# Attention plus two expert layers on one core: queries and keys loaded with doubled rows and split in place, instead of split once and moved by DMA

## The chip, the core and the metric

The kernel runs on one core of one Trainium2 chip. The metric is device time in microseconds (us) of one execution, start to end; lower is better. The engines are named as in the profile: PE (TensorE, matmuls), DVE (VectorE), ACT (ScalarE), POOL (GpSimd) and SP (SyncE, which here issues nearly all DMAs, in order).

## What is computed

The reference, cut to what matters:

```python
# q, k, v: (4, 8, 576, 64): batch, heads, sequence, head size
scores = np.matmul(q, k.transpose(0, 1, 3, 2)) / np.sqrt(64)
thresh = np.max(scores, axis=-1, keepdims=True) - tau
scores = np.where(scores >= thresh, scores, -1000000000.0)
attn = np.exp(scores - np.max(scores, axis=-1, keepdims=True))
attn = attn / (np.sum(attn, axis=-1, keepdims=True) + 1e-09)
x = np.matmul(attn, v)                         # then to (2304, 512)
g = x @ w_gate                                 # 512 -> 1536
x = (g / (1 + np.exp(-g)) * (x @ w_val)) @ w_out
h = np.maximum(x @ w_in, 0.0)                  # 512 -> 2048
x = (h * h) @ w_out2
```

Everything is float32. A matmul in full float32 is replaced by passes over parts: a number is split into a high part, rounded to the format fp32r that PE reads, and a low part, the rest, and the products high x high, high x low and low x high are summed.

## The kernel before

**Stages.** Attention over 4 batches of 8 heads comes first. The heads are taken in 16 pairs, and a pair has nine tiles of 128 queries (ORDER, L642): four of head a, one that holds the last 64 queries of both heads (T), four of head b. That makes 144 tiles. The first layer's gate and value matmuls of finished batches run between the tiles as fill (`work`, L872: every tile adds 2600 columns to a credit that fill may use up; what is left runs on PE alone behind the last tile). Behind that comes the rest of the two layers, which is not touched by the change.

**One tile.** `QK` (L652) multiplies queries with keys into PSUM. A query tile has 128 rows of contraction: 64 rows of high parts of the scaled queries and 64 rows of low parts (`qs`); the keys stand as `kh` (high parts twice) and `kl` (low parts twice), so two matmuls for each half of the 576 keys give all the products. `RED` (DVE) takes the row maximum, `CUT` and `EXP` (ACT) threshold and exponentiate with a row sum, `RCP` (DVE, L696) inverts it, `NORM` (POOL, L700) scales. In batches 1 to 3 NORM writes a 16-bit high part, `LO` (DVE, L751) the low part beside it, `XT` (L759) is a transposing DMA issued on SP, and `AV` (L763) multiplies with the values, fourteen matmuls for each of four parts of a pair. In batch 0 the tiles are transposed on PE and copied by DVE and ACT instead. In batches 1 to 3, `rs`, the reciprocal times a constant, is made by a one-column instruction on POOL right before NORM.

**Buffers.** EXP's results (`es`, L445) turn over three buffers in batch 0 and two in batches 1 to 3, where the third is one of NORM's three 16-bit buffers (`both`, L447).

**A pair's preparation** (`pair_steps`, L586) is a generator that is advanced one step per tile while the pair before is worked on. One load of 896 KB brings q, k and v of both heads into `raw` (one buffer), with 64 rows per head. ACT scales the queries into the high part and copies the keys into theirs (`land`); DVE takes the low queries, POOL the low keys in two halves, in place. Then `move`, once for each head, issues six DMAs on SP that put high and low rows where `qs`, `kh` and `kl` want them, each 64 rows to 64 rows, 144 KB. For head a it also moves the low keys of both heads into one joint tile `kd` and the high queries of the T tile into `qd`, a block diagonal, so that the T tile needs three matmuls a half and not four (L655 to L661). `tail` (L482) copies the T tile's 64 queries from `qs` into `qt` on POOL. `values` (L510) splits the values in batches 1 to 3: POOL copy, POOL subtraction, POOL copy, POOL subtraction for each head.

The first pair (`first_pair`, L524) loads each head's rows twice from a second input and splits in place.

**What sets the order.** The code is emitted tile by tile in the loop at the end; the offsets in the table `early` (L1693) put a step ahead of or behind others. Each engine and SP then work in their fixed order, an instruction waiting for its inputs holding all behind it.

Of the kernel before, what the change touches and what calls it, by code (L numbers as in the profile page):

```python
# [22 lines left out]
P = 128  # L23
# [15 lines left out]
RAWW = 2 * S + 2 * VW  # L39
# [45 lines left out]
def attention_moe(tc, qkv, qk0, tau, w1, w2, out, cfg):  # L85
# [361 lines left out]
    both = [es[-1].bitcast(F16)[:, : 2 * S], *(ptp.tile([P, 2 * S], F16, name=f"both{j}", tag=f"both{j}") for j in range(2))]  # L447
# [17 lines left out]
    qds = [ptp.tile([P, P], F32R, name=f"qd{i}", tag=f"qd{i}") for i in range(1)]  # L465
# [35 lines left out]
    def whole_values(h):  # L501
        hd = heads[h]
        if any(whole(h // 2, i) for i, x in PARTS.items() if x[2] == hd["odd"]):
            c0 = 5 * 640 + h % 4 * (VW + D)
            hd["vf"] = flat[:, c0 : c0 + VW + D]
            c0 += hd["odd"] * D
            a = 2 * S + hd["odd"] * VW
            nc.sync.dma_start(flat[:, c0 : c0 + VW], qkv[h // 2, :, a : a + VW])

    def values(hd, h, raw):  # L510
# [4 lines left out]
        v = raw[:, 2 * S + odd * VW : 2 * S + (odd + 1) * VW].rearrange("p (c d) -> p c d", d=D)  # L515
# [8 lines left out]
    def first_pair():  # L524

        raw = load_pair(0)
        for h in range(2):
            r = raw if h == 0 else rawp.tile([P, 2 * S], F32, name="raw01", tag="land")
            if h:
                for c in (0, S):  # L530
                    nc.sync.dma_start(r[:, c : c + S], qk0[h, :, c : c + S])
            else:

                for c in (slice(0, P), slice(S, 2 * S), slice(P, S)):
                    nc.sync.dma_start(r[:, c], qk0[h, :, c])
# [42 lines left out]
            def s2():  # L578
                tail(hd)
                values(hd, h, raw)  # L580
# [5 lines left out]
    def pair_steps(p):  # L586

        raw = load_pair(p)
        land = rawp.tile([P, 2, S], F32R, name=f"land{p}", tag="land")
        q, k = raw[:, 0:S], raw[:, S : 2 * S]  # L590
        qh, kh = land[:, 0], land[:, 1]

        def move(h):
            hd = head(h)
            rows = slice(hd["odd"] * D, (hd["odd"] + 1) * D)
            for dst, parts_ in (
                (hd["qs"], (qh, q.bitcast(F32R))),
                (hd["kh"], (kh, kh)),
                (hd["kl"], (k.bitcast(F32R), k.bitcast(F32R))),
            ):  # L600
                for j, src in enumerate(parts_):
                    nc.sync.dma_start(dst[j * D : (j + 1) * D, :].bitcast(F32), src[rows, :].bitcast(F32))
            tail(hd)
            if not hd["odd"]:
                hd["qd"], hd["kd"] = qds[0], qp.tile([P, S], F32R, name=f"kd{p}", tag="kd", bufs=1)
                nc.sync.dma_start(hd["kd"].bitcast(F32), k)
                for c in (slice(0, D), slice(D, P)):
                    nc.sync.dma_start(hd["qd"][c, c].bitcast(F32), qh[c, 4 * P : S].bitcast(F32))
# [12 lines left out]
        yield None
        ops.sub(cfg["kl"], k[:, :HS].bitcast(F32R), k[:, :HS], kh[:, :HS].bitcast(F32))
# [29 lines left out]
    def QK(t):  # L652
# [36 lines left out]
    def EXP(t):  # L689
        e = es[t % (len(es) if t < 9 * NPAIR else len(es) - 1)]  # L690
# [221 lines left out]
    for i in range(NTILE + late):  # L912
# [39 lines left out]
        if i == 4:  # L952
            with tc.issue_after(st[2]["norm"]):
                for x_ in qds:
                    nc.gpsimd.memset(x_.bitcast(F32), 0.0)
# [671 lines left out]
def pack(inputs):  # L1627
# [96 lines left out]
```

## Time and profile before

| | |
|---|---|
| median of 3 runs | 1229.49 us (1227.45 to 1229.86) |
| the profiled execution | 1229.54 us; its span from first to last instruction 1227.8 us |
| mean granted PE clock | 0.968 of full |
| busy, share of the span | PE 91%, DVE 72%, ACT 50%, POOL 25% |
| DMA | 179.90 MB, 147 GB/s |

The profile is of one execution. A busy time is that of an engine's instructions without waits; PE's is overstated where matmuls overlap. A wait is charged to what ended it. The granted clock is the share of full speed that PE was given: 1.00 is 2.4 GHz, 0.5 is 1.2 GHz. POOL has no work behind the attention, so its 25% of the span falls into the first 541 us.

### The profile page before, as it was taken

How to read it: one execution, taken by the hardware profiler on the slowest of the kernel's cores; microseconds unless marked ns; L12 is line 12 of the kernel's file. 1: busy time of each engine (PE TensorE's matmuls, PEld its weight loads, DVE VectorE, ACT ScalarE, POOL GpSimd, SP SyncE). 2: the span in 40 equal slices, each digit the busy share in tenths (PEclk: the TensorE clock that was granted, in tenths of full speed). 3: DMA queues.
4: the chain of work that ended last, by engine and by line, in shares of the span. 5: the costliest groups of instructions: out<-in, count | busy, mean ns of one | idle time of the engine just before them, and what ended most of it. 6: DMA issues, size and time to landing. Idle time of an engine off the chain costs nothing.

```text
span 1227.8 us, 18958 instructions
## 1 busy us (share of the span) xinstructions
PE 1113.4 (91%) x6194; PEld 965.7 (79%) x6194; DVE 887.3 (72%) x2088; ACT 615.1 (50%) x1377; POOL 307.8 (25%) x524
## 2 busy tenths in 40 slices
PE   7998877667878877899999999999999999999998
PEld 6776766456667765799888888889889899889997
DVE  7888865765676757659998687878765858867554
ACT  7886644455554545535543343434555545554232
POOL 5577755654555646310000000000000000000000
PEclk9999988789989899999999999999999999999999
DMA  7768867777897787613222013436435444544452
GB/s 209 217 180 201 192 137 157 142 162 160 166 174 169 154 164 159 127 36 99 89 80 85 17 44 120 146 118 223 184 147 185 166 155 158 183 155 151 177 182 92
DMA packets 188258, 179.90 MB, mean 147 GB/s; under 512 B 138112, under 2 KB 139392, under 8 KB 188160
## 3 DMA queue, kind: packets, MB, share of 16 engines
q1 hardware_dynamic: 188016, 178.70, 54.4%
q8 instruction: 49, 0.80, 0.3%
q14 instruction: 49, 0.40, 0.1%
q10 hardware_dynamic: 144, 0.00, 0.0%
HBM read 93.06 MB, written 22.28 MB: 94 GB/s over the span
## 4 chain that ended last, share of the span: by engine, by line
PE 55%; POOL 14%; issue 9%; DMA 8%; DVE 8%; SPq 3%; ACT 3%; POOLq 0%; DVEq 0%; ACTq 0%
PE mm L258 16%; PE mm L1532 15%; PE mm L1479 11%; PE mm L300 7%; DMA raw<-in_qkv_dram 3%; POOL both L707 3%; POOL raw L78 3%; PE bank L258 2%; DMA qs<-raw 2%; POOL e L707 2%; DMA wr<-in_w_dram 2%; PE bank L780 1%; POOL vs L74 1%; POOL rs L706 1%; DVE st__114 L677 1%
## 5 line engine op out<-in xcount | busy, mean ns | idle before, releaser
L677 DVE TENSOR_SCALAR_CACHE_REDUCE st__114<-s,tau_c 128x576 bf16<-128x576 f32 x144 | 116.7, 811 | 36.8 <-PE s L667 25.9
L685 ACT ACTIVATE z<-s,thr 128x576 f32<-128x576 f32 x144 | 106.3, 738 | 48.9 <-DVE st__114 L677 40.6
L693 ACT ACTIVATE e<-z 128x577 f32<-128x577 f32 x144 | 98.5, 684 | 60.0 <-DVE r L698 38.8
L258 PE MATMUL mm<-xs,wa 128*128 128x512 f32 (+2 forms) x672 | 125.7, 347 | 0.5 <-ACT x L70 0.5
L258 PEld LDWEIGHTS mm<-xs,wa 128*128 128x128 f32 x672 | 109.4, 188 | 15.7 <-ACT x L70 0.7
L258 PE MATMUL bank<-xs_m,wa 128*128 128x288 f32 x576 | 100.2, 316 | 19.4 <-DVE xs_m L78 11.6
L780 PE MATMUL bank<-pt,vs 128*128 128x256 f16 (+1 forms) x432 | 76.5, 321 | 40.7 <-DMA pt<-both 21.2
L755 DVE SCALAR_TENSOR_TENSOR both<-e,rs,both 128x512 f16<-128x512 f32 (+1 forms) x144 | 85.6, 635 | 37.5 <-POOL both L707 37.2
L667 PE MATMUL s<-kh,qs 128*128 128x288 f32 x256 | 88.0, 361 | 24.9 <-ACT z L685 14.3
L258 PEld LDWEIGHTS bank<-xs_m,wa 128*128 128x128 f32 x576 | 86.2, 200 | 25.7 <-DVE xs_m L78 13.9
L780 PEld LDWEIGHTS <-vs 128*128 128x128 bf16 x432 | 41.2, 107 | 61.9 <-issue 28.4
L667 PEld LDWEIGHTS s<-kh,qs 128*128 128x128 f32 x256 | 50.5, 200 | 41.4 <-ACT z L685 26.0
L667 PE MATMUL s<-kl,qs 128*128 128x288 f32 x256 | 74.6, 312 | 3.7 <-DMA kl<-raw 3.7
L258 PE MATMUL mm<-xs,wb 128*128 128x512 f32 (+1 forms) x360 | 74.9, 368 | 0.0
L1549 DVE TENSOR_TENSOR xF<-xF,mm 128x512 f32<-128x512 f32 x54 | 36.9, 684 | 51.0 <-PE mm L1532 50.9
L258 PEld LDWEIGHTS mm<-xs,wb 128*128 128x128 f32 x360 | 62.8, 188 | 11.3
L755 DVE SCALAR_TENSOR_TENSOR e<-e,rs,e 128x512 f16<-128x512 f32 x72 | 47.2, 696 | 29.9 <-POOL e L707 29.8
L1532 PE MATMUL mm<-wb,wx 128*128 128x512 f32 x270 | 67.2, 389 | 0.0
L70 ACT ACTIVATE wb<-wf 128x256 fp32r<-128x256 f32 x82 | 34.0, 414 | 65.5 <-DVE wf L1134 38.4
L1479 PE MATMUL mm<-right,wb 128*128 128x384 f32 x348 | 65.3, 335 | 0.8 <-DVE right L78 0.8
L1131 ACT ACTIVATE wf<-wr 128x256 f32<-128x256 f32 x64 | 27.6, 433 | 69.6 <-DMA wr<-in_w_dram 49.3
L1479 PEld LDWEIGHTS mm<-right,wb 128*128 128x128 f32 x348 | 60.8, 188 | 1.5 <-DVE right L78 1.0
(163 smaller groups left out, 2645.7 us busy)
## 6 DMA issues: line engine op xcount, KB each, us to landing
wr<-in_w_dram SPq DMA_DIRECT2D x106, 256.0 KB, 3.0
raw<-in_qkv_dram SPq DMA_DIRECT2D x15, 896.0 KB, 5.9
kh<-land SPq DMA_DIRECT2D x60, 144.0 KB, 2.7
kl<-raw SPq DMA_DIRECT2D x60, 144.0 KB, 2.9
xF<-in_w_dram SPq DMA_DIRECT2D x30, 256.0 KB, 3.2
right<-kept1T SPq DMA_DIRECT2D x8, 768.0 KB, 5.5
right<-kept0T SPq DMA_DIRECT2D x7, 768.0 KB, 5.4
right<-kept SPq DMA_DIRECT2D x6, 768.0 KB, 4.3
```

The lines of the kernel that those rows point to most:

```text
L258: mm(pt[:, :n], w[:, a, col + c * P : col + (c + 1) * P], xs[:, b, c, :], start=(i == 0), stop=(i == len(TERMS) - 1),)
L300: mm(pt[:, :n], ws[k][:, a, 2 * DM + m * P : 2 * DM + (m + 1) * P], us[k][:, b, :], start=(k == 0 and i == 0), stop=(k == ahead and i == 2),)
L667: mm(sp[:, cols], l, r[:, cols], start=(n_ == 0), stop=(n_ == len(pairs) - 1),)
L677: red = nc.vector.tensor_scalar(st_, st[t]["s"][:, :S], scalar1=tau_c, scalar2=None, op0=ALU.subtract, op1=ALU.max, accum_out=th)
L685: nc.scalar.activation(z[:, :S], st[t]["s"][:, :S], AF.Prelu, bias=st[t]["thr"], scale=-1.0, alpha=1 / SLOPE)
L693: ex = nc.scalar.activation(e, st[t]["z"], AF.Exp, scale=-SLOPE, accum_out=sum_)
L707: norm = nc.gpsimd.tensor_scalar(a[:, :S], e, scalar1=rs, scalar2=1.0, op0=ALU.mult, op1=ALU.mult)
L755: nc.vector.scalar_tensor_tensor(a[:, to : to + c.stop - c.start], e[:, c], r, a[:, c], op0=ALU.mult, op1=ALU.subtract)
L780: mm(o[:, :n], v, pt[:, k if k < 9 else k - 9, lo : lo + n], start=(k == 0), stop=(k == 13))
L1479: mm(bank[:, :BK], w[:, a, c * P : (c + 1) * P], t[:, b, c, :], start=(n == 0 and x in ("11", "12", "S1")), stop=(n == 5), skip_group_chec ...
L1532: mm(pt, u[:, b, s * P : (s + 1) * P], w[a], start=(half == 0 and j == 0 and i == 0), stop=(half == 1 and j == 1 and i == 2),)
L1549: nc.vector.tensor_tensor(acc[:, j, :], acc[:, j, :], pt, op=ALU.add)
```

## The change

The host lays out q and k for each head with its 64 rows twice (128 rows of 1152 floats), and v in an input of its own. Each head is loaded by itself, 576 KB, into a buffer of its own, and v of a pair, 320 KB, in batches 1 to 3. The high queries are made on all 128 rows by POOL in batch 0 and by ACT behind it; DVE turns the second 64 rows into low parts; ACT copies the high keys, POOL subtracts the low keys in two halves, for each head and on 128 rows. No DMA moves anything inside the chip; `kd`, `qd` and `land` go, and the T tile has four matmuls a half. EXP has three buffers throughout and NORM three of its own. `rs` is made on DVE behind the reciprocal. The two value copies of a head go from POOL to ACT.

The diff, cut to its core:

```diff
-    both = [es[-1].bitcast(F16)[:, : 2 * S], *(ptp.tile([P, 2 * S], F16, name=f"both{j}", tag=f"both{j}") for j in range(2))]
+    both = [ptp.tile([P, 2 * S], F16, name=f"both{j}", tag=f"both{j}") for j in range(3)]
...
-    def load_pair(p):
-        raw = rawp.tile([P, RAWW], F32, name=f"raw{p}", tag="raw")
-        if p:
-            nc.sync.dma_start(raw, qkv[p])
-        return raw
+    def raw_head(h):
+        return rawp.tile([P, 2 * S], F32, name=f"raw{h}", tag=f"raw{h % 2}")
...
     def pair_steps(p):
...
-        yield None
-        if cfg["qs"] == "A":
-            nc.scalar.activation(qh, q, AF.Copy, scale=qscale)
...
-        ops.sub(cfg["kl"], k[:, HS:].bitcast(F32R), k[:, HS:], kh[:, HS:].bitcast(F32))
-        move(2 * p)
...
+        raws = [raw_head(2 * p + j) for j in range(2)]
+        rawv = None
+
+        def query(j):
+            hd, q = head(2 * p + j), raws[j][:, :S]
+            if p < NPAIR:
+                nc.gpsimd.tensor_scalar(hd["qs"], q, scalar1=qscale, scalar2=1.0, op0=ALU.mult, op1=ALU.mult)
+            else:
+                nc.scalar.activation(hd["qs"], q, AF.Copy, scale=qscale)
+
+        def key(j):
+            hd, q = heads[2 * p + j], raws[j][:, :S]
+            ops.copy(cfg["kh"], hd["kh"], raws[j][:, S:])
+            low = hd["qs"][D:, :]
+            nc.vector.scalar_tensor_tensor(
+                low, q[D:, :], qscale[D:, :], low.bitcast(F32), op0=ALU.mult, op1=ALU.subtract
+            )
+
+        def key_low(j, c):
+            hd = heads[2 * p + j]
+            ops.sub(cfg["kl"], hd["kl"][:, c], raws[j][:, S:][:, c], hd["kh"][:, c].bitcast(F32))
+
+        halves_ = (slice(0, HS), slice(HS, S))
+        nc.sync.dma_start(raws[0], qk[2 * p])
+        yield None
+        nc.sync.dma_start(raws[1], qk[2 * p + 1])
+        if not all(whole(p, i) for i in PARTS):
+            rawv = rawp.tile([P, 2 * VW], F32, name=f"rawv{p}", tag="rawv")
+            nc.sync.dma_start(rawv, values_[p])
+        yield None
+        query(0)
+        yield None
+        key(0)
+        yield None
+        key_low(0, halves_[0])
+        yield None
+        key_low(0, halves_[1])
+        tail(heads[2 * p])
+        yield None
+        values(heads[2 * p], 2 * p, rawv)
+        query(1)
+        yield "next"
+        key(1)
+        key_low(1, halves_[0])
+        yield None
+        key_low(1, halves_[1])
+        tail(heads[2 * p + 1])
+        values(heads[2 * p + 1], 2 * p + 1, rawv)
+        yield None
...
-            pairs = [(hd["qt"][:], hd[x_]) for hd in (ha, hb) for x_ in ("kh", "kl") if x_ == "kh" or "kd" not in ha]
-            if "kd" in ha:
-                pairs.append((ha["qd"], ha["kd"]))
+            pairs = [(hd["qt"][:], hd[x_]) for hd in (ha, hb) for x_ in ("kh", "kl")]
...
-        e = es[t % (len(es) if t < 9 * NPAIR else len(es) - 1)]
+        e = es[t % len(es)]
...
     def RCP(t):
         r = st[t]["r"] = sm.tile([P, 1], F32, name=f"r{t}", tag="r")
         nc.vector.reciprocal(r, st[t]["sum"])
+        if way(t) == "VV":
+            rs = st[t]["rs"] = sm.tile([P, 1], F32, name=f"rs{t}", tag="rs")
+            nc.vector.tensor_scalar(rs, r, scalar1=UNIT, scalar2=None, op0=ALU.mult)
...
-            rs = st[t]["rs"] = sm.tile([P, 1], F32, name=f"rs{t}", tag="rs")
-            nc.gpsimd.tensor_scalar(rs, r, scalar1=UNIT, scalar2=1.0, op0=ALU.mult, op1=ALU.mult)
+            rs = st[t]["rs"]
...
-    "vh": "P",
+    "vh": "A",
```

## Rows read from the trace of the kernel before

**Rows 1.** Windows: length, busy us of PE, weight loads, DVE, ACT, POOL; clock, DMA.
```profile
496.40:514.60 18.20, 15.62 (x107) 13.27 (x108) 14.26 (x39) 12.48 (x27) 9.04 (x19) 1.00 0.67 122
0.00:95.00 95.00, 82.34 (x480) 70.17 (x481) 77.65 (x210) 80.26 (x184) 59.41 (x102) 1.00 0.72 204
95.00:521.00 426.00, 330.33 (x2078) 272.56 (x2077) 295.91 (x699) 223.68 (x498) 243.21 (x415) 0.91 0.79 161
521.00:541.00 20.00, 19.58 (x148) 19.32 (x146) 7.21 (x16) 5.99 (x16) 5.19 (x8) 1.00 0.01 2
541.00:1227.80 686.80, 681.14 (x3492) 603.69 (x3492) 506.50 (x1164) 305.21 (x680) 0.00 (x0) 1.00 0.39 134
```
**Rows 2.** PE in order of time: start, length, line, count.
```profile
364.82 1.77 PE L300 MATMUL bank<-m_u,wa 128*128 128x288 f32 x12
```

**Rows 3.** POOL in order of time: NORM of tiles 36, 135 and 143.
```profile
95.64 0.79 POOL L707 TENSOR_SCALAR both<-e,rs 128x576 f16<-128x576 f32 x1
...
496.40 0.75 POOL L707 TENSOR_SCALAR both<-e,rs 128x576 f16<-128x576 f32 x1
...
514.58 0.75 POOL L707 TENSOR_SCALAR e<-e,rs 128x576 f16<-128x576 f32 x1
```

**Rows 4.** POOL in order of time at the end of a pair.
```profile
377.73 0.74 POOL L707 TENSOR_SCALAR e<-e,rs 128x576 f16<-128x576 f32 x1
...
389.14 0.24 POOL L74 TENSOR_SCALAR qt<-qs 128x64 fp32r<-128x64 f32 x1 [6.37 <-DMA qs<-raw]
...
390.81 0.75 POOL L707 TENSOR_SCALAR both<-e,rs 128x576 f16<-128x576 f32 x1
```

**Rows 5.** SP's queue in order of time, the same stretch.
```profile
381.56 1.24 SPq L602 DMA_DIRECT2D kl<-raw  x2
...
386.50 0.59 SPq L602 DMA_DIRECT2D qs<-raw  x1
```

**Rows 6.** Waits, 95 to 521 us: who for whom, total us, times, longest.
```profile
POOL rs L706 <- DVE r L698: 78.7, 72, 2.6
...
POOL qt L74 <- DMA qs<-raw: 50.0, 8, 9.1
```

**Rows 7.** ACT by line and shape, 95 to 521 us: busy us, mean ns, idle before.
```profile
L70 ACT ACTIVATE xs_m<-xF 128x288 fp32r<-128x288 f32 x21 | 8.6, 431 | 3.8 <-PE bank L258 3.8
L612 ACT ACTIVATE land<-raw,qscale 128x576 fp32r<-128x576 f32 x11 | 8.5, 773 | 7.7 <-DMA raw<-in_qkv_dram 7.0 <-issue 0.6
...
L70 ACT ACTIVATE land<-raw 128x576 fp32r<-128x576 f32 x11 | 7.4, 669 | 0.0
```

**Rows 8.** DVE and POOL by line and shape, the same columns.
```profile
L618 DVE SCALAR_TENSOR_TENSOR raw<-raw,qscale,land 128x576 fp32r<-128x576 f32 x11 | 10.8, 980 | 4.1 <-ACT land L612 4.1
...
L547 DVE SCALAR_TENSOR_TENSOR qs<-raw,qscale,qs 64x576 fp32r<-64x576 f32 x1 | 0.8, 818 | 0.0
...
L536 DVE TENSOR_SCALAR qscale<-tau_t 128x1 f32<-128x1 f32 x1 | 0.2, 153 | 1.7 <-DMA tau_t<-in_tau_dram 1.7
...
L706 POOL TENSOR_SCALAR rs<-r 128x1 f32<-128x1 f32 x108 | 23.1, 213 | 82.1 <-DVE r L698 78.7 <-ACT e L693 1.9 <-ACT z L685 1.1
...
L78 POOL TENSOR_TENSOR raw<-raw,land 128x288 fp32r<-128x288 f32 x22 | 22.0, 1018 | 0.0
...
L561 POOL TENSOR_SCALAR qs<-raw,qscale 128x576 fp32r<-128x576 f32 x1 | 0.7, 746 | 3.1 <-DMA raw<-in_qk_dram 3.1
```

**Rows 9.** DVE's LO in the last pair; LO and POOL's key-low subtractions earlier, by time.
```profile
502.24 0.95 DVE L755 SCALAR_TENSOR_TENSOR e<-e,rs,e 128x512 f16<-128x512 f32 x2 [0.43 <-POOL e L707]
...
372.60 2.03 DVE L755 SCALAR_TENSOR_TENSOR both<-e,rs,both 128x512 f16<-128x512 f32 x2 [0.61 <-POOL both L707]
...
372.53 2.02 POOL L78 TENSOR_TENSOR raw<-raw,land 128x288 fp32r<-128x288 f32 x2
```

**Rows 10.** ACT's EXP in the last pair, by time.
```profile
503.30 0.69 ACT L693 ACTIVATE e<-z 128x577 f32<-128x577 f32 x1 [0.47 <-DVE r L698]
```

More of the change, by code (lines that the diff above doesn't have):

```diff
@@ L38 @@
 VW = 5 * D
-RAWW = 2 * S + 2 * VW
 TAU_MAX = 80.0
@@ L82, in split, with attention_moe @@
         self.sub(elo, lo, src, hi.bitcast(F32))
-def attention_moe(tc, qkv, qk0, tau, w1, w2, out, cfg):
+def attention_moe(tc, qk, values_, tau, w1, w2, out, cfg):
     nc = tc.nc
@@ L464, in attention_moe @@
         qts.append(t)
-    qds = [ptp.tile([P, P], F32R, name=f"qd{i}", tag=f"qd{i}") for i in range(1)]
     heads = {}
-    def load_pair(p):
-        raw = rawp.tile([P, RAWW], F32, name=f"raw{p}", tag="raw")
-        if p:
-            nc.sync.dma_start(raw, qkv[p])
-        return raw
+    def raw_head(h):
+        return rawp.tile([P, 2 * S], F32, name=f"raw{h}", tag=f"raw{h % 2}")
     def head(h):
@@ L506, in whole_values, with values @@
             c0 += hd["odd"] * D
-            a = 2 * S + hd["odd"] * VW
-            nc.sync.dma_start(flat[:, c0 : c0 + VW], qkv[h // 2, :, a : a + VW])
-    def values(hd, h, raw):
+            a = hd["odd"] * VW
+            nc.sync.dma_start(flat[:, c0 : c0 + VW], values_[h // 2, :, a : a + VW])
+    def values(hd, h, raw=None):
         odd = hd["odd"]
@@ L514, in values @@
             return
-        v = raw[:, 2 * S + odd * VW : 2 * S + (odd + 1) * VW].rearrange("p (c d) -> p c d", d=D)
+        v = raw[:, odd * VW : (odd + 1) * VW].rearrange("p (c d) -> p c d", d=D)
         vs = hd["vs"] = qp.tile([P, 5, P], BF16, name=f"vs{h}", tag="vs", bufs=3)
@@ L524, in first_pair @@
     def first_pair():
-        raw = load_pair(0)
         for h in range(2):
-            r = raw if h == 0 else rawp.tile([P, 2 * S], F32, name="raw01", tag="land")
+            r = raw_head(h)
             if h:
                 for c in (0, S):
-                    nc.sync.dma_start(r[:, c : c + S], qk0[h, :, c : c + S])
+                    nc.sync.dma_start(r[:, c : c + S], qk[h, :, c : c + S])
             else:
                 for c in (slice(0, P), slice(S, 2 * S), slice(P, S)):
-                    nc.sync.dma_start(r[:, c], qk0[h, :, c])
+                    nc.sync.dma_start(r[:, c], qk[h, :, c])
                 nc.vector.tensor_scalar(qscale, tau_t, scalar1=0.0, scalar2=0.125, op0=ALU.is_ge, op1=ALU.mult)
@@ L579, in s2 @@
                 tail(hd)
-                values(hd, h, raw)
+                values(hd, h)
             yield s0
@@ L586, in pair_steps @@
     def pair_steps(p):
[L588 to L608, printed above, removed]
+        raws = [raw_head(2 * p + j) for j in range(2)]
@@ L623, in pair_steps @@
         yield None
-        ops.sub(cfg["kl"], k[:, HS:].bitcast(F32R), k[:, HS:], kh[:, HS:].bitcast(F32))
-        move(2 * p)
+        key_low(0, halves_[1])
+        tail(heads[2 * p])
         yield None
-        values(heads[2 * p], 2 * p, raw)
+        values(heads[2 * p], 2 * p, rawv)
+        query(1)
         yield "next"
-        move(2 * p + 1)
+        key(1)
+        key_low(1, halves_[0])
         yield None
-        values(heads[2 * p + 1], 2 * p + 1, raw)
+        key_low(1, halves_[1])
@@ L951, in attention_moe @@
             at_(av_parts, 3, name="AV")
[L952 to L955, printed above, removed]
         at_(mp1.flush, "P", name="FP")
@@ L1630, in pack @@
     q, k, v = (np.asarray(inputs[n]) for n in "qkv")
-    qkv = np.zeros((B * NPAIR, P, RAWW), np.float32)
-    qkv[:, :, 0:S] = q.reshape(B * NPAIR, 2, S, D).transpose(0, 1, 3, 2).reshape(-1, P, S)
-    qkv[:, :, S : 2 * S] = k.reshape(B * NPAIR, 2, S, D).transpose(0, 1, 3, 2).reshape(-1, P, S)
+    q, k = (x.reshape(B * H, S, D).transpose(0, 2, 1) for x in (q, k))
+    qk = np.concatenate([np.concatenate([x, x], axis=1) for x in (q, k)], axis=2)
     vv = v.reshape(B * NPAIR, 2, S, D)
-    full = qkv[:, :, 2 * S :].reshape(B * NPAIR, P, 2, 5, D)
+    full = np.zeros((B * NPAIR, P, 2, 5, D), np.float32)
     full[:, :, :, :4] = vv[:, :, : 4 * P].reshape(B * NPAIR, 2, 4, P, D).transpose(0, 3, 1, 2, 4)
@@ L1638, in pack @@
     full[NPAIR:, D:, :, 4] = full[NPAIR:, :D, :, 4]
-    qkv[:, :, 2 * S :] = full.reshape(B * NPAIR, P, 2 * VW)
     def bits(w):
@@ L1657, in pack @@
     return [
-        ("in_qkv_dram", np.ascontiguousarray(qkv)),
-        ("in_qk0_dram", np.stack([np.concatenate([qkv[0, r : r + D, : 2 * S]] * 2) for r in (0, D)])),
+        ("in_qk_dram", np.ascontiguousarray(qk)),
+        ("in_v_dram", full.reshape(B * NPAIR, P, 2 * VW)),
         ("in_tau_dram", np.ascontiguousarray(tau)),
```

7 lines of the change are left out of this document (removed).

## The prediction

> **What bounds the kernel now.** I first read the stages by windows [rows 1]. From 541 us to the end TensorE (PE) is busy 681 of 687 us at full clock; the change touches nothing there, so that part stays. The attention of batches 1 to 3, from 95 to 521 us, is different: PE is busy 330 of 426 us at a mean granted clock of 0.91, DVE 296, ACT 224, POOL 243. No engine is full, so waits hold the stage. It has 2078 matmuls; twelve in a row take 1.77 us including the tail of the last, about 0.3 [rows 2], so one costs 0.134 us and all of them 278 us. Some 148 us of the stage are slack or low clock on PE.
>
> Which wait it is shows in GpSimd's (POOL's) order of time. The instruction of NORM for tile 36 starts at 95.64 us, for tile 135 (first of the last pair) at 496.40, for tile 143 at 514.58 [rows 3]. So eleven pairs of heads took 400.8 us, **36.4 us each**, while the last pair, during which no further pair is loaded, moved or split, made its eight steps in 18.2 us: 2.27 us a tile, **20.4 us for nine**. It also has less fill: 107 matmuls [rows 1] where a mean pair has 2078 / 12 = 173.
>
> The same view at the end of a pair [rows 4]: a NORM at 377.73, the next at 390.81. In between POOL stood 6.37 us before `qt`, a small copy that needs the moved queries; NORM is behind it in POOL's order, LO on DVE behind NORM, the transposing DMA behind LO. SP's queue shows why the move is late [rows 5]: at 381.56 it still issues low keys of the first head, then the joint key and query, and the second head's queries only at 386.50. The table of waits counts 50.0 us in 8 such waits [rows 6].
>
> **The change, part by part**, for each of the eleven pairs prepared in batches 1 to 3 unless said.
>
> *Removed.* Twelve moves of 144 KB, one of 288 KB, two of 16 KB: 15 issues on SP, and with them `qt`'s wait on a DMA. `qt` then follows a scaling and a subtraction. I let the old preparation go as a whole, by starting from the last pair's 20.4 us, and add the new work to it. That is a choice, made because that pair alone shows the loop bare.
>
> *Loads.* One transfer of 896 KB becomes two of 576 and one of 320 in buffers of their own, each free as soon as its head is split. SP has 3 issues for 16, and by the sizes 2 MB a pair leave and 0.6 MB come, at a DMA share of 0.79 [rows 1]. Cost nothing; the cover is a load four steps or more ahead of its split. If that is gone, a load that waits on SP for its buffer holds the transposing DMAs behind it, and AV on PE waits for those.
>
> *ACT.* One scaling (773 ns) and one key copy (669) more, and four value copies of 320 columns taken from POOL [rows 7]. That shape stands nowhere; between 288 columns (431) and 576 (669) it is about 0.46 us. Sum 1.44 + 1.83 = 3.3 us. In the last pair ACT waits 0.47 us a tile [rows 10], 4.2 us over nine, so between 0 and 3.3 us reach the path; I take half, 1.6, as the copies come in a clump and the second copy of a head waits for a subtraction on POOL.
>
> *DVE.* The low queries go from one instruction (980 ns) to two of 64 rows x 576 at 818 [rows 8]: 1.6 us against the last pair, which has none, all on the path, since DVE idles only 0.43 us a step there, at LO waiting for NORM [rows 9]. `rs` leaves POOL (213 ns and some 0.1 to the next instruction) for DVE, 153 ns by the only one-column scaling it has [rows 8]: minus 0.15 us a tile, 1.3 a pair, with bounds of 0 and 2.7.
>
> *POOL.* Key lows go from two halves of 1018 ns to four; four value copies and `rs` leave, and POOL waits 78.7 us for reciprocals anyway [rows 6]: its own time costs nothing. But it slows DVE. LO takes 0.95 us alone and took 2.03 beside two key-low halves [rows 9]: 0.54 us for each subtraction met. A pair will have eight of them (four key, four value): 4.3 us at most, 0 at least. I take 4.3, because DVE is the engine of the loop.
> SBUF — State Buffer, section SBUF: two separate sides, in the Trainium skill has a harder rule: the port pair that DVE and GpSimd share is locked for a whole instruction, and the loser fully blocks, where DVE has two SBUF inputs. By it each subtraction could hold DVE for all of its length; the sum by that is a rival below. In rows 9 the loss was about half of it, so the row is taken.
>
> *E buffers.* EXP turns over three buffers instead of two; its wait of 0.47 us in rows 10 ends where LO frees one. Bounds 0 and 4.2 us; DVE's loop stands behind it, so I take 0.
>
> *PE.* The fifth tile of a pair has eight matmuls for six: 2 x 0.134 = 0.27 us. And a mean pair has 66 matmuls more than the last, 8.8 us, against 18.2 - 107 x 0.134 = 3.9 us free there: by PE alone a pair is near 20.4 + 4.9 = 25.3 us. That is a floor beside DVE's sum, not on top of it.
>
> *Batch 0.* Three prepared pairs. Query scaling goes to POOL (two of 746 ns [rows 8]), with two key-low halves more; PE, DVE and ACT are 0.82 to 0.87 busy there [rows 1]. Added at most 3 x (0.27 PE + 0.65 DVE + 1.1 port) = 6 us; the moves that leave may give some back. I take plus 4, bounds minus 5 and plus 10.
>
> **The sum.** A pair by DVE's loop: 20.4 + 1.6 (ACT) + 1.6 - 1.3 (DVE) + 4.3 (port) + 0.3 (PE) = 26.9 us. PE's 25.3 is so close that they will at times meet in order; I take 28. Gain 11 x (36.4 - 28) = 92 us, less 4 for batch 0: 88. Fill is handed out by tile, not by time, so the 20 us of PE-only fill behind the last tile (521 to 541 [rows 1]) stay. The profiled run took 1229.54 us (span 1227.8), the median is 1229.49, so nothing is to be corrected: **1229.5 - 88 = 1141 us**.
>
> **The rivals.**
> *All of it hides (0.15).* PE is the bound: 25 us a pair, gain 11 x 11.4 - 4 = 121: 1108 us. For it: the clock is 1.00 wherever PE is dense [rows 1]. Against it: DVE needs about as much.
> *ACT takes POOL's place (0.18).* The second value copy of each head waits on ACT for a subtraction that stands on POOL behind a NORM; CUT and EXP are behind it in order. If that costs each of two heads a tile step (2.2 us), a pair is 32.4: gain 44 - 4, 1190 us. For it: ACT starts every tile. Against it: it is busy 224 of 426 us.
> *The port is paid in full (0.08).* Eight subtractions at 1.0 us [rows 9], not 0.54: 3.8 us more, a pair of 31.8: gain 51 - 4, 1183 us. For it: LO rows that double. Against it: half of each meets nothing.
> *It is slower (0.04).* The same place as ACT's case at a higher price: copies hold EXP, EXP the reciprocal, that NORM, and the subtraction stands behind NORM. It decides from (36.4 - 28) / 2 = 4.2 us a head, about two tile steps. At 6 us a head a pair is 40: 1229.5 + 40 + 4 = 1273 us. Against it: copies and subtractions alternate within POOL already.
> *The gap stays (0.05).* Not the move but the PE work that runs there (AV, fill) holds the end of a pair; `qt` is early and NORM still has no tile. Only `rs` is gained, 11 x 1.3, less 4: 1219 us, and at a poorer sum no change. Against it: the row before `qt` names the DMA.
>
> **How the numbers follow.** The forecast has 0.50, its own range 26 to 30.5 us a pair, 1119 to 1169. With most of the first three rivals the range is 1100 to 1192; the slow case, the gap that stays and the far ends, 0.18, are left out. About 0.2% (2.5 us) is what a measurement of this kernel can tell from no change. Faster by more than that: the forecast, the first three rivals and most of the last, 0.94; within it 0.02; slower 0.04.
>
> **What would show it.** Right: no wait of `qt` on a DMA; NORM steps of 2 to 3.5 us across the ends of pairs; the last NORM near 426 us; a granted clock near 1.0 before it; DMA share about 0.65; a tail of fill as long as now. Wrong: steps over 6 us still at pair ends; ACT waiting for POOL at value copies; LO often at 2 us; loads waiting on SP in front of transposes; a stage behind the tail that is more than shifted.

## The result, and the profile after

The changed kernel takes **1175.09 us** (median of 4 runs, 1173.16 to 1175.94) against 1229.67 us for the kernel before in the same comparison: a ratio of 0.9557, 95% interval [0.9539, 0.9574]. That is 54.6 us less, where 88 were forecast. It lies inside the range, 6 us above the forecast's own 1119 to 1169. The profiled execution has a span of 1174.1 us (1227.8 before), a gain of 53.7, and the places below are read from it.

First the windows of the changed kernel, with the same columns as [rows 1]: batch 0, the attention of batches 1 to 3, the tail of fill, the rest, and the eight steps of the last pair.

```profile
0.00:104.00 104.00, 85.79 (x489) 71.88 (x490) 86.31 (x221) 86.29 (x203) 74.64 (x118) 1.00 0.46 146
104.00:463.00 359.00, 300.93 (x2055) 264.66 (x2054) 313.24 (x808) 245.01 (x548) 214.85 (x278) 0.94 0.67 136
463.00:488.00 25.00, 25.00 (x192) 24.51 (x189) 8.22 (x19) 6.74 (x19) 5.19 (x8) 1.00 0.06 11
488.00:1174.10 686.10, 680.81 (x3494) 603.84 (x3492) 506.38 (x1164) 305.66 (x681) 0.00 (x0) 1.00 0.40 134
...
433.20:459.80 26.60, 22.76 (x162) 20.67 (x161) 24.00 (x61) 15.84 (x38) 12.61 (x16) 0.94 0.53 90
```

The rest is 0.7 us shorter, as good as untouched. In the second row DVE is now busy 313 of 359 us (87%), where it was 296 of 426. PE is at 301 of 359 and still waits. So the stage has moved from "nobody is full" to "DVE is nearly full". The DMA share falls from 0.79 to 0.67 and not further: what is gone are the moves of the preparation, while the transposing DMAs, one for each tile of these batches, still run from SBUF to SBUF. The last row answers to the first of [rows 1]: the same eight steps, 18.2 us before, now take 26.6 and hold 162 matmuls for 107.

POOL in order of time gives the marks that answer to [rows 3]: NORM of tile 36, of tiles 134 and 135 in one row of two, and of tile 143. The two rows between are NORM of tiles 107 and 108, on either side of the pair end of [rows 4].

```profile
104.72 0.73 POOL L705 TENSOR_SCALAR both<-e,rs 128x576 f16<-128x576 f32 x1
...
341.74 0.74 POOL L705 TENSOR_SCALAR both<-e,rs 128x576 f16<-128x576 f32 x1 [1.40 <-DVE rs L697]
343.96 0.74 POOL L705 TENSOR_SCALAR both<-e,rs 128x576 f16<-128x576 f32 x1 [1.48 <-ACT vs L69]
...
432.43 1.47 POOL L705 TENSOR_SCALAR both<-e,rs 128x576 f16<-128x576 f32 x2
...
459.77 0.74 POOL L705 TENSOR_SCALAR both<-e,rs 128x576 f16<-128x576 f32 x1 [1.04 <-DVE both L753]
```

Tile 135 starts at about 433.2 (the second of the row's two). The eleven pairs took 433.2 - 104.7 = 328.5 us, **29.9 us each**, where 36.4 was measured before and 28 forecast. The 13 us hole between two NORMs of [rows 4] is gone: at the same place they start 2.22 us apart, and over all eleven ends of pairs the step is 2.5 us on the mean (0.7 to 5.6), where it was 10.5 (4.8 to 13.1). The whole span then splits so (us, by NORM):

| stretch | before | after | difference | forecast |
|---|---|---|---|---|
| start to tile 36 | 95.6 | 104.7 | +9.1 | +4 |
| eleven pairs, tiles 36 to 135 | 400.8 | 328.5 | -72.3 | -92.4 |
| last eight steps | 18.2 | 26.6 | +8.4 | 0 |
| tile 143 to the rest | 26.4 | 28.2 | +1.8 | 0 |
| the rest | 686.8 | 686.1 | -0.7 | 0 |

The shortfall of 34.7 us is 20.1 in the pairs, 8.4 in the last steps, 5.1 in batch 0 and 1.8 in the tail, less 0.7.

The waits of the changed kernel from 102.0 to 428.9 us (who for whom, total us, times, longest):

```profile
PE s L663 <- ACT z L681: 43.4, 34, 3.6
POOL both L705 <- DVE rs L697: 31.2, 27, 2.1
DVE both L753 <- POOL both L705: 30.2, 51, 1.7
ACT z L681 <- DVE r L694: 24.8, 14, 4.5
ACT z L681 <- DVE st__115 L673: 24.5, 29, 2.1
POOL qt L73 <- DVE qs L596: 16.5, 9, 2.8
ACT vs L69 <- POOL rawv L77: 14.4, 11, 3.3
```

`qt` waits for no DMA any more. What is left is the ring of the loop itself, PE for CUT on ACT, ACT for RED and the reciprocal on DVE, DVE for NORM on POOL, and POOL for `rs` on DVE. The last row is the place of the rival in which ACT takes POOL's place: it exists, eleven times, at 14.4 / 11 = 1.3 us each.

DVE by line and shape in the same stretch (busy us, mean ns, idle before):

```profile
L753 DVE SCALAR_TENSOR_TENSOR both<-e,rs,both 128x512 f16<-128x512 f32 x97 | 92.7, 956 | 31.3 <-POOL both L705 30.2
...
L753 DVE SCALAR_TENSOR_TENSOR both<-e,rs,both 128x64 f16<-128x64 f32 x97 | 41.1, 424 | 0.0
L596 DVE SCALAR_TENSOR_TENSOR qs<-raw,qscale,qs 64x576 fp32r<-64x576 f32 x22 | 20.2, 917 | 1.0 <-ACT qs L590 0.3
...
L697 DVE TENSOR_SCALAR rs<-r 128x1 f32<-128x1 f32 x98 | 14.6, 149 | 1.3
...
L287 DVE SCALAR_TENSOR_TENSOR m_th<-m_th,bank 128x288 f32<-128x288 f32 x23 | 10.3, 448 | 0.8 <-PE bank L257 0.5
L278 DVE SCALAR_TENSOR_TENSOR m_th<-m_th,bank 128x288 f32<-128x288 f32 x23 | 10.2, 444 | 0.3 <-ACT m_th L277 0.2
...
L77 DVE TENSOR_TENSOR xs_m<-xF,xs_m 128x288 fp32r<-128x288 f32 x17 | 8.0, 496 | 0.0
```

Low queries cost 20.2 / 11 = 1.8 us a pair (1.6 in the sum) and `rs` 149 ns (153). The last three rows are work of the fill: (10.3 + 10.2 + 8.0) / 11 = **2.6 us of DVE a pair**, which the sum does not have.

### The profile page after: what moved, and what is told of

It is laid out like the page before. It is cut to its first block, busy times and chain, and to the rows that moved or that the text cites. A ratio compares the mean times of both kernels' runs of the same rounds, so it can differ in the third digit from the quotient of the medians.

```text
span 1174.1 us, 18645 instructions
## 1 busy us (share of the span) xinstructions
PE 1092.5 (93%) x6224; PEld 964.9 (82%) x6224; DVE 914.1 (78%) x2211; ACT 643.7 (55%) x1449; POOL 294.7 (25%) x403
## 4 chain that ended last, share of the span: by engine, by line
PE 54%; DVE 8%; ACT 3%; DMA 2%; issue 2%; POOL 2%; ACTq 0%; SPq 0%; POOLq 0%; DVEq 0%
PE mm L257 17%; PE mm L1526 15%; PE mm L1473 11%; PE mm L299 7%; DMA wr<-in_w_dram 2%; DVE both L753 2%; PE bank L257 2%; DVE st__115 L673 1%; POOL both L705 1%; PE bank L299 1%; ACT z L681 1%; DVE h L1460 1%; DVE wa L77 1%; PE bank L778 1%; DVE xF L793 0%
## 5 line engine op out<-in xcount | busy, mean ns | idle before, releaser
L753 DVE SCALAR_TENSOR_TENSOR both<-e,rs,both 128x512 f16<-128x512 f32 x216 | 139.1, 686 | 36.3 <-POOL both L705 35.0
L681 ACT ACTIVATE z<-s,thr 128x576 f32<-128x576 f32 x144 | 106.2, 737 | 71.6 <-DVE r L694 29.7
L705 POOL TENSOR_SCALAR both<-e,rs 128x576 f16<-128x576 f32 x108 | 88.4, 820 | 74.6 <-DVE rs L697 35.1
L257 PE MATMUL bank<-xs_m,wa 128*128 128x288 f32 x576 | 95.0, 314 | 3.8 <-DVE xs_m L77 1.9
L778 PE MATMUL bank<-pt,vs 128*128 128x256 f16 (+1 forms) x432 | 66.1, 297 | 2.7 <-DVE xF L793 1.4
L1460 DVE TENSOR_TENSOR h<-mm,h 128x384 f32<-128x384 f32 x72 | 39.6, 551 | 30.3 <-PE mm L1473 30.3
```

Source lines behind the costliest of these rows:

```text
L257: mm(pt[:, :n], w[:, a, col + c * P : col + (c + 1) * P], xs[:, b, c, :], start=(i == 0), stop=(i == len(TERMS) - 1),)
L681: nc.scalar.activation(z[:, :S], st[t]["s"][:, :S], AF.Prelu, bias=st[t]["thr"], scale=-1.0, alpha=1 / SLOPE)
L705: norm = nc.gpsimd.tensor_scalar(a[:, :S], e, scalar1=rs, scalar2=1.0, op0=ALU.mult, op1=ALU.mult)
L753: nc.vector.scalar_tensor_tensor(a[:, to : to + c.stop - c.start], e[:, c], r, a[:, c], op0=ALU.mult, op1=ALU.subtract)
L778: mm(o[:, :n], v, pt[:, k if k < 9 else k - 9, lo : lo + n], start=(k == 0), stop=(k == 13))
L1460: return ("D", read(lambda: nc.vector.tensor_tensor(h, bank[:, :BK], h, op=ALU.add), bank))
```

## The experiments

Each experiment is compared with the kernel before on the same chip. "Pair" is the mean of eleven, from the start of EXP (ACT) of tile 36 to that of tile 135; it is 36.45 us before and 29.72 after.

| run | edited kernel | us | ratio, 95% interval | EXP of tile 36 at | pair |
|---|---|---|---|---|---|
| the change itself | | 1175.09 | 0.9557 [0.9539, 0.9574] | 102.0 | 29.72 |
| first value copy held | after | 1172.26 | 0.9534 [0.9514, 0.9554] | 99.8 | 29.78 |
| `rs` on POOL | after | 1188.52 | 0.9666 [0.9644, 0.9687] | 101.5 | 31.03 |
| key lows on DVE | after | 1168.45 | 0.9503 [0.9482, 0.9524] | 100.5 | 29.57 |
| no key lows | after | 1157.09 | 0.9409 [0.9384, 0.9435] | 102.1 | 28.35 |
| two E buffers | after | 1177.21 | 0.9588 [0.9573, 0.9602] | 102.4 | 30.03 |
| value copies on POOL | after | 1186.24 | 0.9659 [0.9645, 0.9673] | 103.9 | 30.66 |
| `qt` copies last | before | 1227.88 | 0.9997 [0.9985, 1.001] | 94.6 | 36.50 |
| moves on ACT's queue | before | 1289.46 | 1.0513 [1.0496, 1.0531] | 114.8 | 38.73 |
| no fill between tiles | after | 1260.03 | 1.0251 [1.0207, 1.0294] | 102.2 | 26.66 |
| no fill between tiles | before | 1340.64 | 1.0905 [1.087, 1.094] | 93.6 | 34.80 |
| `qt` behind NORM | before | 1229.35 | 1.0004 [0.9986, 1.0022] | 94.1 | 36.31 |
| held copy and key lows on DVE | after | 1168.72 | 0.9508 [0.9474, 0.9542] | 98.2 | 29.67 |

**Batch 0: the first value copy.** ACT in order of time at the start of the changed kernel:

```profile
12.55 0.83 ACT L69 ACTIVATE vs<-rawv 128x320 bf16<-128x320 f32 x2 [6.93 <-DMA rawv<-in_v_dram]
13.28 0.72 ACT L681 ACTIVATE z<-s,thr 128x576 f32<-128x576 f32 x1
...
14.30 0.67 ACT L689 ACTIVATE e<-z 128x577 f32<-128x577 f32 x1
```

CUT of the first tile stands behind copies of values that AV needs only in batch 1, and these wait 6.93 us for their load. EXP of that tile starts at 14.30 us (8.9 before). The edit holds the first copy of each head until EXP of the second tile of the pair before has been issued:

```diff
-        ops.copy(cfg["vh"], v1, v)
+        with tc.issue_after(st[9 * (h // 2) - 8]["exp"]):
+            ops.copy(cfg["vh"], v1, v)
```

> The changed kernel, with the first value copy of each head held on ACT behind the EXP of the second tile of the pair before. In the changed kernel ACT stands 6.9 us at the very start before the value load of pair 4, which is needed only at 105 us. If that wait is what made batch 0 longer (first tile 6.4 us later), the time falls by 5 to 7 us, from 1175 to about 1169. If batch 0 is longer because of POOL's added scalings and subtractions, it stays within 2 us.

EXP of the first tile went back to 9.1 us, but EXP of tile 36 only from 102.0 to 99.8, and the time fell by 2.8 us, between the two expectations. The intervals overlap, but each run with the edit is below each run of the changed kernel (at most 1172.8 against at least 1173.2). The late start is real, yet most of it was made up inside batch 0 anyway. The other 6 us of batch 0 are not explained by it.

**The loop: `rs` back on POOL.**

```diff
-        if way(t) == "VV":
-            rs = st[t]["rs"] = sm.tile([P, 1], F32, name=f"rs{t}", tag="rs")
-            nc.vector.tensor_scalar(rs, r, scalar1=UNIT, scalar2=None, op0=ALU.mult)
...
-            rs = st[t]["rs"]
+            rs = st[t]["rs"] = sm.tile([P, 1], F32, name=f"rs{t}", tag="rs")
+            nc.gpsimd.tensor_scalar(rs, r, scalar1=UNIT, scalar2=1.0, op0=ALU.mult, op1=ALU.mult)
```

> The changed kernel, with rs back on POOL in front of NORM. Theory D (DVE's work sets the pace in batches 1 to 3, it is busy 313 of 359 us): 108 instructions of 149 ns leave DVE, the time falls by 8 to 16 us, to about 1163. Theory L (the loop of reciprocal, NORM and LO sets it, as in the clean steps before the change): the loop gets 0.15 to 0.3 us a tile longer, the time rises by 10 to 25 us, to about 1190.

It cost 13.4 us: the pair went from 29.72 to 31.03, 1.31 us for nine tiles. In this run's window and waits, from 101.5 to 442.8 us, DVE stands longer for NORM (30.2 in the changed kernel) and ACT longer for DVE (24.5 and 24.8):

```profile
101.50:442.80 341.30, 278.65 (x1877) 242.30 (x1875) 286.10 (x649) 227.96 (x510) 226.97 (x362) 0.94 0.65 136
```

```profile
DVE both L751 <- POOL both L703: 47.4, 69, 2.5
ACT z L681 <- DVE st__115 L673: 46.8, 36, 3.9
ACT z L681 <- DVE r L694: 36.6, 23, 3.7
```

A step of the loop that is 0.15 us longer would give this nine times over, and it comes although DVE has one instruction a tile less: DVE is busy 84% of the stretch, for 88% in the changed kernel. But POOL is busy 2.4 us a pair more as well, and the longer step and the fuller POOL were not separated.

**The port: key lows on DVE, and left out.** Two runs, the first with the four subtractions of a pair on DVE, the second without them in pairs 5 to 15 (there QK reads the high keys in place of the low ones: the low part of the keys is missing from the scores, and no matmul less runs).

```diff
-    "kl": "P",
+    "kl": "D",
```

> The changed kernel, with the key-low subtractions on DVE instead of POOL (62 of 455 ns, 28 us of DVE work, about 20 in batches 1 to 3). If POOL's two-input subtractions cost DVE only little, theory D says plus 15 to 25 us, to about 1195. If each takes half a microsecond from LO or its neighbours (44 x 0.54 = 24 us in batches 1 to 3), it comes out even, 1170 to 1182.

```diff
         def key_low(j, c):
             hd = heads[2 * p + j]
+            if p > NPAIR:
+                hd["kl"] = hd["kh"]
+                return
```

> The changed kernel without the key-low subtractions of pairs 5 to 15: those 44 instructions are left out, and QK reads the high keys in the place of the low ones, so scores are not the reference's. It measures what the subtractions cost by standing beside DVE. Theory D with the port: LO's mean falls towards 0.95 us for both of its parts, the time falls by 15 to 24 us, to about 1155. Theory L or a bound on PE: less than 6 us.

DVE's LO and the moved subtractions in the first of the two, from 100.5 to 425.8 us:

```profile
L753 DVE SCALAR_TENSOR_TENSOR both<-e,rs,both 128x512 f16<-128x512 f32 x98 | 89.6, 915 | 21.6 <-POOL both L705 19.7
...
L753 DVE SCALAR_TENSOR_TENSOR both<-e,rs,both 128x64 f16<-128x64 f32 x98 | 34.0, 347 | 0.0
L77 DVE TENSOR_TENSOR kl<-raw,kh 128x288 fp32r<-128x288 f32 x43 | 22.7, 529 | 0.1
```

The window of that run, and the same subtractions on POOL in the changed kernel, from 102.0 to 428.9 us:

```profile
100.50:425.80 325.30, 277.60 (x1865) 239.29 (x1865) 297.36 (x792) 231.69 (x521) 170.59 (x223) 0.94 0.71 147
```

```profile
L77 POOL TENSOR_TENSOR kl<-raw,kh 128x288 fp32r<-128x288 f32 x44 | 41.3, 955 | 10.9 <-ACT kh L69 10.9
```

And LO in the second, from 102.1 to 413.9 us:

```profile
L756 DVE SCALAR_TENSOR_TENSOR both<-e,rs,both 128x512 f16<-128x512 f32 x98 | 88.7, 905 | 29.6 <-POOL both L708 28.6
...
L756 DVE SCALAR_TENSOR_TENSOR both<-e,rs,both 128x64 f16<-128x64 f32 x98 | 34.1, 348 | 0.0
```

Without the subtractions the time falls by 18.0 us, 0.41 us for each of the 44; the pair falls by 1.37 us, 0.34 each. LO's two instructions take 1.25 us a tile for 1.38, some 1.1 us a pair. Yet on DVE the same work is dearer than what it took from LO (22.7 / 11 = 2.1 us a pair against about 1.1), and still the run is 6.6 us faster than the change, below both expectations. Only 1.7 of these 6.6 are in the eleven pairs (11 x 0.15). EXP of tile 36 is 1.4 us earlier and the eight steps behind tile 135 are 3.1 shorter (24.4 for 27.5). So LO's slowing is not all that POOL's subtractions cost; they also stand in POOL's order ahead of NORM, but these parts were not separated. DVE is busy 91% of the stretch in this run, so the 88% of the changed kernel was no ceiling.

**E buffers.** EXP over two buffers in batches 1 to 3 instead of three:

```diff
-        e = es[t % len(es)]
+        e = es[t % (len(es) if t < 9 * NPAIR else len(es) - 1)]
```

> The changed kernel, with EXP over two buffers in batches 1 to 3, as before the change. My sum took the third buffer as worth 0, since DVE stands behind it: within 5 us of 1175. If EXP's lead is what lets the tiles overlap, plus 15 to 40 us.

It took 2.1 us more, and the pair is 30.03 us for 29.72. The two intervals just touch, and each run with the edit is above each run of the changed kernel (at least 1176.4 against at most 1175.9). So the third buffer is worth little, some 2 us.

**ACT: value copies back on POOL.**

```diff
-    "vh": "A",
+    "vh": "P",
```

> The changed kernel, with the value copies back on POOL. Theory C (the clump of copies on ACT, each second one waiting for a subtraction, holds the tiles): the time falls by 10 to 20 us, to about 1160. Theory D: ACT waits for DVE anyway (69 us before its thresholds), POOL has room, so within 5 us, with up to 7 us less because the early wait for the value load leaves ACT.

It is slower by 11.2 us, which neither theory had, and the pair is 30.66. So the copies cost less on ACT than on POOL; what they cost on ACT was not measured by itself. This run's waits of ACT from 97 to 440 us still have CUT behind DVE's reciprocal (24.8 in the changed kernel, in a stretch 5% shorter):

```profile
ACT z L681 <- DVE r L694: 37.8, 16, 4.8
...
ACT z L681 <- DVE st__115 L673: 27.6, 28, 2.3
```

**What held the end of a pair before.** Three edits of the kernel before. In the first, both `qt` copies of a pair are emitted at the end of its preparation:

```diff
-            tail(hd)
             if not hd["odd"]:
...
+        tail(heads[2 * p])
+        tail(heads[2 * p + 1])
         values(heads[2 * p + 1], 2 * p + 1, raw)
```

> The kernel before, with both copies into qt emitted at the end of a pair's preparation instead of right behind each head's moves. If POOL's wait in qt holds NORM, as I wrote, the gaps at pair ends shrink and the time falls by 20 to 60 us. If the first tile of the next pair waits for its own keys, which the moves bring late, NORM has nothing to do in the gap and the time stays within 8 us of 1229.

Nothing moved, but it tells nothing: POOL's order at the end of a pair came out nearly the same, and its waits still hold the line "POOL qt" behind the DMA with 50.0 us in 8. In the second the moves are issued from ACT's queue:

```diff
-                    nc.sync.dma_start(dst[j * D : (j + 1) * D, :].bitcast(F32), src[rows, :].bitcast(F32))
+                    nc.scalar.dma_start(dst[j * D : (j + 1) * D, :].bitcast(F32), src[rows, :].bitcast(F32))
```

> The kernel before, with the twelve moves of a pair issued from ACT's queue instead of SP's. If the moves are late because they stand in SP's order among the transposing DMAs (each of which waits for LO), the gap at pair ends shrinks and much of the change's gain is had with the moves still there: minus 20 to 60 us. If the transfers themselves are the cost, or ACT suffers by as much, within 15 us of 1229.

It is 5% slower, outside both expectations, and already by 21 us at tile 36. The twelve issues a pair now stand in ACT's order among CUT and EXP; that this is what costs was not tested, and the question of SP's order is not answered. The third moves only the second head's `qt` copy behind NORM of the next pair's first tile:

```diff
+        with tc.issue_after(st[9 * p]["norm"]):
+            tail(heads[2 * p + 1])
```

> The kernel before with one thing moved: the second head's small copy of 64 queries (qt) stands on POOL behind NORM of the next pair's first tile, not ahead of it, so that NORM no longer stands behind a copy that waits for a moved query. Theory Q (the prediction's: qt's wait holds NORM and by it LO, the transposing DMA and AV): 20 to 60 us faster, pair 31 to 34.5 us, and the table of waits has the 50 us no longer. Rival K (the first tile of the next pair waits for its own moved keys, the last of which land some 3 us after SP issued them at the end of the pair, so NORM has no tile before that, and qt's wait only lies beside it): within 8 us of the kernel before, pair 35.8 us or more.

The time is 1229.35, the same. POOL in order of time at the same end of a pair as [rows 4]:

```profile
378.94 0.74 POOL L709 TENSOR_SCALAR e<-e,rs 128x576 f16<-128x576 f32 x1
...
391.71 0.19 POOL L708 TENSOR_SCALAR rs<-r 128x1 f32<-128x1 f32 x1 [7.73 <-DVE r L700]
392.00 0.74 POOL L709 TENSOR_SCALAR both<-e,rs 128x576 f16<-128x576 f32 x1
392.71 0.24 POOL L74 TENSOR_SCALAR qt<-qs 128x64 fp32r<-128x64 f32 x1
```

`qt` stands behind NORM and waits for nothing, and between the two NORMs there are still 13.06 us (13.08 in [rows 4]). POOL now waits for the reciprocal instead. The step from the last tile of a pair to the next pair's first, by EXP, is 12.88 us, and was 12.80. PE of the kernel before, in order of time, shows what came late at that end:

```profile
381.48 0.50 PE L667 MATMUL s<-kh,qs 128*128 128x288 f32 x2 [2.40 <-DMA kh<-land]
...
386.19 0.37 PE L667 MATMUL s<-kl,qs 128*128 128x288 f32 x1 [0.19 <-DMA kl<-raw]
```

These are the first tile's own high and low keys, moved by the same queue [rows 5]. With this tile's scores complete only some 387 us from the start, there is no NORM before RED, CUT, EXP and the reciprocal have followed, at 390.81 [rows 4]. That the keys and not another moved part hold every such end is argued from this order, and not shown by a run of its own.

**Fill.** All fill is put behind the last tile, in both kernels:

```diff
-        fstate["credit"] += cfg["rate"]
+        fstate["credit"] += cfg["rate"] if not i else 0
```

> The changed kernel with no fill between the tiles of the attention: tiles add no credit, and all of the first layer's gate and value matmuls of batches 1 to 3 run on PE behind the last tile. Nothing is left out; the whole run will be longer, by what the fill no longer hides (some 60 us or more), and only the pair time counts (EXP of tile 36 to EXP of tile 135, over eleven; 29.7 us now). Theory M (the sum left out the fill's work on DVE: the last pair, its base, has little fill, and over a mean pair m_th and xs_m take some 2.8 us of DVE): the pair falls to 26 to 27.7 us, near the sum of 26.9. Rival L (the loop from EXP to LO and the clumps of preparation set the pair, fill lies beside it): the pair stays at 29 us or more. Rival P (PE is the bound): it falls to 25 us or less.

> The kernel before with the same edit: no fill between tiles, all of it behind the last tile. Only the pair time counts (36.45 us now, a gap at the end of each pair in it). If the moves by DMA hold the end of a pair (queries or keys that land late): the gap stays, the pair is 33 us or more. If the gap were PE's own work (AV and fill) at that place, as the prediction's last rival says: the pair falls to 22 to 27 us. The whole run is longer by what the fill no longer hides.

The window of the eleven pairs of the changed kernel:

```profile
102.00:428.90 326.90, 273.97 (x1862) 240.49 (x1860) 287.13 (x741) 228.35 (x511) 200.74 (x262) 0.94 0.68 142
```

The same without fill:

```profile
102.20:395.50 293.30, 198.96 (x1053) 142.89 (x1052) 262.27 (x681) 214.01 (x455) 175.77 (x214) 0.81 0.76 156
```

And the kernel before without fill:

```profile
93.60:476.30 382.70, 230.78 (x1052) 159.76 (x1049) 239.61 (x582) 189.60 (x403) 196.61 (x346) 0.71 0.81 170
```

In the changed kernel the pair falls by 3.06 us to 26.66, though PE's granted clock is 0.81 there and not 0.94, so that what PE still does takes longer (a mean of 0.35 us for AV's matmuls, 0.30 with fill). PE is no bound: 809 matmuls less, 108 us at 0.134, took 34 us from the eleven pairs. DVE's busy time falls by (287.13 - 262.27) / 11 = 2.26 us a pair, and its share of the stretch stays, 88% with fill and 89% without. But the edit also takes 6.8 us of busy time a pair from PE, 2.3 from POOL (`m_u` is copied and subtracted there) and 1.3 from ACT. That the 3.06 us are the fill's is shown; that they come through DVE is argued from DVE being the fullest, and POOL's part was not separated. Before, without fill, the pair is still 34.80 and the step at its end 11.61 us: the gap was not the fill.

**Both gains together.**

```diff
-        ops.copy(cfg["vh"], v1, v)
+        with tc.issue_after(st[9 * (h // 2) - 8]["exp"]):
+            ops.copy(cfg["vh"], v1, v)
...
-    "kl": "P",
+    "kl": "D",
```

> The changed kernel with two edits that each gained alone: the first value copy of a pair is held on ACT until EXP of the tile eight after that pair's preparation began (alone 1172.3 us), and the four low-key subtractions go from POOL to DVE (alone 1168.5 us). If the two gains are of different places (the first tiles of batch 0; POOL's slowing of DVE in every pair), they add: 1165 to 1167 us. If both came from the same place: about 1168.5 us.

They do not add: 1168.72 against 1168.45 for the key lows on DVE alone. EXP of tile 36 is 2.3 us earlier than there, and the pairs give 1.1 of it back (11 x 0.10). These two are the fastest seen that leave nothing out, some 6.5 us below the change.

## Why the prediction was right and where it was wrong

**The direction and the mechanism.** That the moves hold the ends of pairs, and that the time comes back when they go, was right: by EXP the step at the end of a pair fell from 12.80 to 2.74 us. It stays at 2.8 to 3.7 us when `rs`, the third buffer or the value copies are put back, so it is the new preparation that closed the gap (moves gone and loads in buffers of their own; these two were not tried apart). Those three are not small, however: put back one by one they cost 13.4, 2.1 and 11.2 us, so that, if they add (which was not run), about half of the 54.6 us is theirs. And of the 10.06 us of the step the other eight steps gave back 3.33 (23.65 before, 26.98 after), and that is where the sum was short.

**`qt` was the wrong victim.** The step "In between POOL stood 6.37 us before `qt` [...] NORM is behind it in POOL's order" is contradicted: with `qt` out of NORM's way nothing changed. The table of waits had counted 50 us for an engine that had no NORM to do yet. The number of the forecast did not rest on it, since the whole old preparation was let go at once. Had the change been only to move `qt`, the same reading would have promised up to 50 us and got none.

**The base had too little fill: the step that failed.** "That is a floor beside DVE's sum, not on top of it" counted the missing fill of the last pair on PE alone. Fill also brings DVE work (`m_th`, `xs_m`), 2.6 us a pair by the rows above, and POOL work (`m_u`); the base has one such DVE instruction, 0.5 us, and only two of AV's five additions on DVE. Without fill the changed kernel's pair is 26.66 us, beside the sum's 26.9; with fill 29.72. The forecast allowed 1.1 for what meets, and the fill cost 3.06, by way of DVE as far as the busy times tell, with POOL's part open. By NORM the pair is 29.9 us for 28, and that is 20 of the 34.7 us that were missed. The floor by PE was off too: it set the 107 matmuls of eight steps against the 173 of nine tiles. On nine tiles it is about 23 us and not 25.3, so PE was not as close as the sum took it.

**The port term was counted partly twice.** 4.3 us a pair was LO's slowing. After the change LO's two instructions take 0.956 + 0.424 = 1.38 us a tile; undisturbed they take 0.750 + 0.276 = 1.03 in the same count (the 0.95 of [rows 9] is the time from the start of the first to the end of the second, which overlap). That is 9 x 0.35 = 3.2 us a pair. But the base had some of it. DVE's groups of LO in the last pair of the kernel before, by the tile that they write:

```profile
L755 DVE SCALAR_TENSOR_TENSOR both<-e,rs,both 128x512 f16<-128x512 f32 x6 | 4.7, 776 | 3.0 <-POOL both L707 3.0
...
L755 DVE SCALAR_TENSOR_TENSOR both<-e,rs,both 128x64 f16<-128x64 f32 x6 | 2.2, 371 | 0.0
L755 DVE SCALAR_TENSOR_TENSOR e<-e,rs,e 128x512 f16<-128x512 f32 x2 | 1.5, 750 | 0.9 <-POOL e L707 0.9
...
L755 DVE SCALAR_TENSOR_TENSOR e<-e,rs,e 128x64 f16<-128x64 f32 x2 | 0.6, 276 | 0.0
```

That is 1.15 us for six tiles and 1.03 for two, 0.8 us over nine more than undisturbed, so 2.4 us were due and not 4.3. So the agreement of 26.66 with 26.9 is in part two errors that cancel (the port too dear; AV's additions, the lower clock and a wait on ACT too cheap), and is no proof of each term.

**The other terms.** `rs` was put at -1.3 us a pair, and putting it back cost 1.31. The E buffers were taken as 0 and are worth 0.3 us a pair, 2.1 us in the whole run. For ACT 1.6 was taken: ACT's wait for POOL's subtraction is 1.3 us a pair, though how much of it reaches the end was not measured. "Its own time costs nothing", of POOL, does not hold: with the value copies back, POOL is busy 1.9 us a pair more and the pair is 0.94 us longer, though ACT has less to do. The four-matmul tile cannot be seen beside the rest.

**The last pair was taken as it stood.** The sum let "eight steps in 18.2 us" and the tail be. They grew by 8.4 and 1.8 us. The window shows 162 matmuls for 107, and 55 at 0.134 are 7.4 us. AV has 56 there for 28, and the fill 78 for 53. In the kernel before, PE ran the other 28 of AV between 484.6 and 493.7 us, in the gap at the end of the pair ahead. What filled a gap has to run somewhere when the gap closes.

**Batch 0** cost 9.1 us for 4, near the stated bound of 10. The copy that waits for its load explains 2 to 3 of them, and that wait was not foreseen: the prediction listed the value copies for batches 1 to 3 only, while pair 4's are issued at the very start. With the value copies on POOL the first EXP is back at 8.9 us, and tile 36 still comes at 103.9. The rest stays open.

**The rivals.** "All of it hides" fell: the pair is 29.7 us and not 25, and PE waits in it. "ACT takes POOL's place" gave 1190 us and comes closer to 1175 than the forecast does, but its price fell: ACT's wait there is 1.3 us a pair where it had 4.4, and taking the copies off ACT made it slower. "The port is paid in full" gave 1183 us, the nearest number of all, by a port that costs more than the forecast's, where the runs show less. It rests on the rule of SBUF — State Buffer, section SBUF: two separate sides, in the Trainium skill, that the shared port is locked for the whole of an instruction. Here the subtractions take about 0.95 us each and leaving them out gained 0.34 to 0.41 each, so on the average less than half of one is lost. By the start and end of each instruction in the eleven pairs, the 35 of LO's 97 larger instructions that no POOL instruction overlaps take 0.74 to 0.75 us, and the 39 that overlap subtractions alone 1.14 on the mean. So LO is slowed where it meets a subtraction, by 0.39 us on the mean; whether the port is locked for a whole instruction the runs do not show. "The gap stays" fell with the change itself and with the fill: the step at a pair's end in the kernel before is 11.61 us without it.

**The signs named beforehand.** `qt`'s wait on a DMA is gone, NORM steps across the ends of pairs by 2.5 us on the mean (2 to 3.5 named, though single ones are 0.7 and 5.6), the DMA share is 0.67 (0.65), and LO takes 1.38 us a tile and not 2. Against it stand the last NORM at 459.8 us (426), a granted clock of 0.94 (1.0) and a tail of 25 us of fill (20). Two signs of being wrong are there in small: ACT waits for POOL at value copies, and loads wait on SP for their buffers, some 28 us over the eleven pairs. Neither shows as the limit: in the changed kernel AV on PE waits for no transposing DMA there.

## What to carry to other kernels

A stretch of the kernel that shows the loop "bare" is a good base only after its work has been compared engine by engine with the stretch it stands for: what is missing counts on every engine that takes part, above all on the one that will be the bound. A long wait in the table names the instruction that waits and not what the wait costs; before it is priced, look whether the work queued behind it could have started, here whether the next NORM had its tile. And where a change closes a gap, ask which engine used the gap for work that was due, since that work comes back later.

## What was not expected of the hardware

Moving a subtraction from POOL, where it takes 955 ns, to DVE, where it takes 529, made the kernel faster although DVE was the fullest engine: 22.7 us of instructions came to it in the eleven pairs, 10 us of busy time net of what LO saved, and the run took 6.6 us less. And PE's granted clock, which the prediction expected to rise to near 1.0 once the gaps were gone, was a mean of 0.94 over the pairs of the changed kernel, where PE was busy 274 of 327 us, and 0.81 without fill, where it was busy 199 of 293; in the kernel before without fill it was 0.71 (231 of 383). Each is a mean over time at 2.4 and at 1.2 GHz. So the run without fill paid some of what it won back in clock, and 3.06 us a pair is rather too little than too much for the fill; how much was not measured.
